# One planned order for a gated S4D convolution and spectral filter: fixed places in SBUF and PSUM, every instruction listed by the kernel, convolution pairs over 128 lanes

## The chip, the cores and the metric

The kernel runs on one core of a Trainium2 chip. Five engines work side by side: TensorE (PE, with its weight loads as PEld), VectorE (DVE), ScalarE (ACT), GpSimd (POOL) and SyncE (SP, which here only issues DMAs). Each runs its own instructions strictly in the order in which they stand in the program, and waits on semaphores for the others. The metric is the time of one execution on the device, in microseconds (us).

## The reference

Two branches are computed from one input `u` (1 x 2048 x 640) and mixed by a gate. In numpy's words, cut to what matters:

```python
g = sigmoid((x * gate_w).sum(-1))                       # one gate per time step
A = -exp(log_A_real) + 1j * A_imag                      # 640 channels x 128 states
P = exp((A * dt)[:, :, None] * arange(2048))            # powers of each state
K = 2 * einsum("dn,dnl->dl", (C_real + 1j*C_imag) * dt, P).real
a = irfft(rfft(u_t, 4096) * rfft(K, 4096))[:, :2048] + u * D_skip
b = irfft2(rfft2(x) * (w_r + 1j * w_i), s=(2048, 640))  # global filter
out = g * a + (1 - g) * b
```

## The kernel before

All Fourier transforms are matrix products with tables. The kernel has these stages; the letters are used below.

- **A** (`phase_a`, first half): for each of four column groups `c` (160 channels), `stage1` (L353, 80 products of 128 columns) and `stage2` (L366, 66 products of 160 columns) give the spectrum of `u`, which goes to DRAM as `u_d` (L448). L435 adds the gate's sums.
- **P** (`phase_p`): DVE and POOL compute the parameters of the 640 x 128 states, split them into three bf16 parts and write them to DRAM (`px_d`, `py_d`, `pm_d`).
- **K** (`phase_b`): the response of the state space model, in 40 tiles, in 8 blocks of 5. A tile takes two magnitude products (`mags`, L686) and two exponentials (L688), two sets of turns (`phases`, L696, six bf16 products of 512 columns) with two sines (L703 for the outer turns, L715 in place in PSUM for the inner ones), POOL products `y` (L706), three DVE products `x` (L718, L719, L720) and 32 small products `p_k` (`kgen`, L735). ACT changes its table between exponentials and sines, so that each block has one stretch of exponentials and one of sines. The turns and magnitudes share two double banks of PSUM (`bank2`), so that the five inner turns of a block use the two in turn.
- **F** (`phase_a`, second half, from L462): the two-dimensional filter, 9 rounds, each with a load of `u_d`, transposes (L533), products (L487, L492), the DVE's product with the filter (`filt`), and the way back (L598), ending in `s3e_d` in DRAM.
- **C** (`phase_c`, `phase_d`): for each column group, `stage1` and `stage2` of K (L353, L366), products with `u_d` on DVE (`ma`, `mb`, L830, L831), their sums `t2` (L835, L836), the way back (L849), a trip through DRAM (`s3_d`, written at L858, read by `load_c` at L901 as tile `t3`, four loads of 32 partitions that are four apart), and the last step: L170 for F's part, L928 for C's part, with the gate on DVE.

A product of the way back has 128 rows: `t2` holds the real part on partitions 0 to 63 and the imaginary part on 64 to 127. DVE and POOL make it out of `ma` and `mb`, whose partitions hold two values of k, in four instructions over 64 partitions each (L835, L836).

Order: tile pools give and take buffers, and generators are merged by shares of time (`merge`, L240, L978): A, F and the first part of C in one stream, P and K in the other; F begins when A has ended and C's main part when K has ended. DMAs are issued from SP, ACT (L817, L858) and POOL (L290, L663 to L671, L936). `t3`, `t3e`, `u` and the other tiles are separate buffers.

Of the kernel before, what the change touches and what calls it, by code (L numbers as in the profile page):

```python
# [11 lines left out]
I32 = mybir.dt.int32  # L12
# [11 lines left out]
NP = 33  # L24
MAGIC = 12582912.0
# [3 lines left out]

# [13 lines left out]
def _tables():  # L51
# [34 lines left out]
    w3 = np.swapaxes(w2, 1, 2) * wk[:, None, None]  # L86
    w2[K0, 64:] = 0.0
# [79 lines left out]
def halved(nc, out, w, x):  # L167

    for i in (0, 64):
        nc.tensor.matmul(out[i:i + 64], w[:, i:i + 64], x, start=True, stop=True)  # L170


def merge(*streams):

    live = [[0.0, t, g] for t, g in streams]
    while live:
        s = min(live, key=lambda x: x[0] / x[1])
        try:
            s[0] += next(s[2])
        except StopIteration:  # L180
            live.remove(s)
# [831 lines left out]
```

## Time and profile before

| | us |
|---|---|
| median of 3 runs (636.74 to 640.0) | 639.94 |
| the profiled execution | 637.14 |
| its span, first to last instruction | 635.3 |
| PE busy in the span | 535.0 (84%) |
| DVE busy | 452.3 (71%) |
| ACT busy | 310.5 (49%) |
| POOL busy | 313.7 (49%) |

The mean clock that TensorE was granted is 0.937 of full speed; 101.84 MB pass through the DMA queues. By the timeline, the first exponential's table load stands at 59.0 us, F works from 147 to 374 us, the last product of K ends at 468.2 us and the last L849 at 617.9 us. A view of windows gives the busy time of each engine in a stretch; a view of lines groups equal instructions with their total and mean time; the timeline gives single rows with their start.

### The profile page before, as it was taken

Reading aid. Unit: us, or ns where it says so; the run is one execution under the profiler, and the core shown is the slowest. Engines: PE = TensorE matmul, PEld = TensorE weight load, DVE = VectorE, ACT = ScalarE, POOL = GpSimd, SP = SyncE. Lnnn points to the kernel's source line nnn. Section 1 sums busy time; section 2 is a strip of 40 time slices with the busy share of each in tenths; the row PEclk is TensorE's granted clock in tenths of the full one; section 3 lists DMA queues with packets and bytes.
Section 4 is the critical chain, followed back from the end, with each engine's and each line's share of the span. In section 5 each row is a group of like instructions: output and inputs, shape, how many; then the busy total and the mean of one; then the engine's idle time right before and its main releaser. Section 6 shows DMA issues by size and latency. Waiting matters only on the chain. (4 is left out here: it accounts for less than half of the span.)

```text
span 635.3 us, 17319 instructions
## 1 busy us (share of the span) xinstructions
PE 535.0 (84%) x7432; PEld 379.6 (60%) x7432; DVE 452.3 (71%) x684; ACT 310.5 (49%) x476; POOL 313.7 (49%) x345
## 2 busy tenths in 40 slices
PE   8696999979984998498998978666687999999875
PEld 6594667647653775265665646333376878876651
DVE  6991487479999798489669705242479698796965
ACT  4564634524871486445773876848531323222120
POOL 4975561563585144803292374170724346546533
PEclk9897999989996799889899999887789999999999
DMA  9776223354354134021420258200044889969767
GB/s 344 301 267 245 79 90 118 114 171 142 86 192 120 42 101 141 8 79 44 162 78 24 63 175 311 94 2 2 1 152 156 300 272 309 359 202 324 255 217 269
DMA packets 49332, 101.84 MB, mean 160 GB/s; under 512 B 4756, under 2 KB 34216, under 8 KB 47624
## 3 DMA queue, kind: packets, MB, share of 16 engines
q1 hardware_dynamic: 24888, 67.08, 30.7%
q10 hardware_dynamic: 20080, 22.52, 11.1%
q0 software_dynamic: 4288, 11.15, 5.3%
q8 instruction: 58, 0.95, 0.6%
q14 instruction: 18, 0.15, 0.1%
HBM read 60.91 MB, written 39.81 MB: 159 GB/s over the span
## 5 line engine op out<-in xcount | busy, mean ns | idle before, releaser
L706 POOL TENSOR_TENSOR y<-e,sc 128x512 f32<-128x512 f32 x80 | 106.3, 1359 | 40.8 <-ACT sc L703 40.7
L366 PE MATMUL p_s<-t,w 128*64 128x160 f32 x1056 | 94.4, 317 | 9.8 <-ACT ut L400 5.4
L366 PEld LDWEIGHTS p_s<-t,w 128*64 128x64 f32 x1056 | 76.6, 140 | 23.9 <-ACT ut L400 6.3
L735 PE MATMUL p_k<-x,y 128*32 128x64 f32 x2560 | 58.9, 239 | 35.4 <-DVE x L719 28.4
L696 PE MATMUL p_p<-tr,pxy 64*128 64x512 bf16 x480 | 77.3, 410 | 6.6 <-ACT sc L703 4.5
L735 PEld LDWEIGHTS p_k<-x,y 128*32 128x32 f32 x2560 | 46.2, 120 | 54.9 <-issue 39.9
L718 DVE SCALAR_TENSOR_TENSOR x<-e,p_p 128x512 f32<-128x512 f32 x40 | 27.3, 682 | 61.9 <-ACT p_p L715 61.8
L688 ACT ACTIVATE e<-p_e 128x1024 f32<-128x1024 f32 x80 | 62.3, 816 | 9.1 <-PE p_e L686 5.8
L715 ACT ACTIVATE p_p<-p_p 128x1024 f32<-128x1024 f32 x40 | 40.4, 1010 | 39.4 <-PE p_p L696 32.9
L354 ACT COPY t<-p_s 128x512 f32<-128x512 f32 x40 | 24.9, 621 | 66.8 <-PE p_s L353 41.2
L835 POOL TENSOR_TENSOR t<-ma 64x320 f32<-64x320 f32 x32 | 28.0, 876 | 54.4 <-DVE ma L830 52.3
L703 ACT ACTIVATE sc<-p_p 128x1024 f32<-128x1024 f32 x40 | 40.5, 1024 | 19.7 <-PE p_p L696 13.0
L720 DVE TENSOR_TENSOR x<-e,p_p 128x1024 f32<-128x1024 f32 x40 | 48.6, 1215 | 0.0
L849 PE MATMUL p_i<-t,w 128*64 128x160 f32 x528 | 43.2, 303 | 4.4 <-POOL t L836 3.4
L353 PE MATMUL p_s<-c,kt 128*64 128x128 f32 x640 | 43.2, 274 | 3.8 <-DVE mb L831 2.0
L353 PEld LDWEIGHTS p_s<-c,kt 128*64 128x64 f32 x640 | 37.9, 136 | 13.4 <-issue 8.2
L589 POOL TENSOR_TENSOR qq<-z 128x320 f32<-128x320 f32 x17 | 16.9, 992 | 57.3 <-DVE z L586 56.0
L696 PEld LDWEIGHTS <-pxy 64*128 64x128 bf16 x480 | 22.4, 98 | 38.0 <-issue 29.0
L849 PEld LDWEIGHTS p_i<-t,w 128*64 128x64 f32 x528 | 37.0, 138 | 9.3 <-POOL t L836 4.0
L353 PE MATMUL p_s<-c,u 128*64 128x128 f32 x640 | 41.5, 277 | 0.2 <-DMA u<-in_u_l 0.2
L851 ACT COPY s<-p_i 128x640 f32<-128x640 f32 x32 | 21.7, 693 | 39.5 <-PE p_i L849 34.6
L353 PEld LDWEIGHTS p_s<-c,u 128*64 128x64 f32 x640 | 35.8, 137 | 6.8 <-issue 5.0
(159 smaller groups left out, 1066.9 us busy)
## 6 DMA issues: line engine op xcount, KB each, us to landing
u_d<-ut SPq DMA_DIRECT2D x32, 320.0 KB, 3.6
us<-u_d ACTq DMA_DIRECT2D x16, 640.0 KB, 6.4
s_d<-s ACTq DMA_DIRECT2D x15, 640.0 KB, 6.3
t<-s_d SPq DMA_DIRECT2D x14, 640.0 KB, 5.6
ww<-in_w_l SPq DMA_DIRECT2D x8, 642.0 KB, 3.9
ue<-u_d SPq DMA_DIRECT2D x8, 640.0 KB, 4.3
k_d<-kt SPq DMA_DIRECT2D x4, 1280.0 KB, 4.7
kt<-k_d SPq DMA_DIRECT2D x8, 640.0 KB, 5.6
```

The lines of the kernel that those rows point to most:

```text
L353: nc.tensor.matmul(p[64 * ri:64 * ri + 64, j, :], src(i + j), e1[ri], start=True, stop=True)
L366: ins = nc.tensor.matmul(p[64 * j:64 * j + 64, i, 160 * ri:160 * ri + 160], w2[:, x, 64 * ri:64 * ri + 64], t1[:, x // 2 if x < 32 else K0 ...
L688: st.exp = S.activation(ef[:, :, c:c + n], p[:, :, :n], AF.Exp)
L696: P.matmul(p[:, h, :], pars[t][1][l, v], turns[v][l, s], start=s == 0, stop=s == 2)
L703: T.trig = st.trig = S.activation(sc.rearrange("p v (h d) i -> p h v (d i)", h=2), p.rearrange("p h (v c) -> p h v c", v=2), AF.Sin, scale ...
L706: G.tensor_tensor(out=y[:, v], in0=es[t][:, :, 64:96], in1=sc[:, 1 - v], op=ALU.mult)
L715: T.trig = st.trig = S.activation(p[:, :, :], p[:, :, :], AF.Sin, scale=TWO_PI)
L718: V.scalar_tensor_tensor(out=x[:, 1, :, 32:64], in0=e[:, :, 32:64], scalar=-1.0, in1=sc[:, 0], op0=ALU.mult, op1=ALU.mult)
L720: V.tensor_tensor(out=x[:, 0].rearrange("p d (h j) -> p d h j", h=2), in0=e[:, :, 0:64].rearrange("p d (h j) -> p d h j", h=2), in1=sc[:, ...
L735: P.matmul(st.pb[32 * r:32 * r + 32, o, :], y[:, ri, 4 * qq + JR[r], :], x[:, ri, 4 * qq + JR[r], :], start=t % 2 + qq + 1 - ri == 0, stop ...
L835: (G if j else V).tensor_tensor(out=t2[0:64, o, :], in0=ma[l, :hn, 0, :], in1=ma[l, :hn, 1, :], op=ALU.subtract)
L849: T.mm = P.matmul(p[x:x + 64, i // 2, 160 * (i % 2):160 * (i % 2) + 160], T.w3[:, k0 + h + i, x:x + 64], t2[:, h + i, :], start=True, stop ...
```

## The change

The kernel is written anew around a planner. All buffers are slices of one SBUF tile `sb` of 53200 words a partition and one PSUM tile `ps` of 8 banks, at places fixed by the program (`Pool`, `Space`, `Banks`). The engines' calls are recorded (`Plan`, `Engine`) with what each reads and writes; `order` lays all of them out in time by estimates of their lengths, greedily and by the longest way to the end, and `emit` issues them in that order. `merge` and the waits on an instruction of another stream are gone. The framework below, which puts in the semaphores, is the same; it now sees every buffer as a part of `sb` or `ps`.

What is computed in each stage stays, with these differences:

- All DMAs are issued from SP.
- The turns of cosines and sines come from one layout of 52 rows (`pp_d` in the place of `px_d` and `py_d`); they are products as before. A tile's outer and inner turns now follow each other, and with two double banks (`pair`) taken in turn, the outer ones always use banks 3 and 4 and the inner ones banks 5 and 6.
- C's way back takes pairs over 128 lanes: `t2` is made by two DVE instructions over 128 partitions (L988, L989), and the product has tiles of 64 rows by 64 columns, 16 for a pair of k in the place of 8 of 128 rows (L997, with its table `t_w3c`). POOL has no part in C any more.
- F's part of the output is gated on ACT, an image row at a time (L1017), C's part on DVE (L1033); both take their PSUM from one bank (`bl`, bank 7). `t3` is one buffer at a fixed place (`t3p`); its four loads are L1024.

The diff, cut to its core (of the planner, its choice of the next instruction):

```diff
-            ga, gl = chain(phase_a(tc, A, T), phase_c(tc, A, T, cctx)), left()
-            next(gl)
-            next(ga)
-            next(gl)
-            while T.pin is None:
-                next(ga)
-            merge((194.0, ga), (76.8, gl))
-            phase_d(tc, A, T, cctx, out)
...
+        sb = top.enter_context(tc.tile_pool(name="sb", bufs=1)).tile([128, WIDE], F32, name="sb")
...
+        R = Plan(tc, sb[:, :], ps[:, :, :])
...
+        Y.dma_start(c1[:, 0:256], A["t_c1"][:, 0:256])
+        columns_head(T, A)
+        Y.dma_start(c1[:, 256:nc1], A["t_c1"][:, 256:nc1])
+        R.tag = "P"
+        params(T, A)
+        R.tag = "A"
+        columns(T, A)
+        R.tag = "K"
+        responses(T, A)
+        R.tag = "F"
+        spectral(T, A)
+        R.tag = "C"
+        convolution(T, A, out)
+        R.emit(order(R.units, OPT))
...
+    def emit(self, order):
+        with self.tc.manual_schedule():
+            for u in order:
+                for p, f, a, k in u.calls:
+                    p(f, a, k)
...
+    rank = {u: u.tail + bias.get(u.tag, 0.0) for u in units}
...
+    while len(out) < len(units):
...
+            s = [(start(u), u) for u in r]
+            s0 = min(x[0] for x in s)
+            lim = max(s0, free[e]) + slack.get(e, 100.0)
+            pick = None
+            for x, u in s:
+                if x > lim:
+                    continue
+                v = rank[u] - (x - s0)
+                if e == "PE" and u.mode != mode:
+                    v -= opt.get("hold", 300.0)
+                if e == "ACT" and u.table and u.table != table:
+                    v -= opt.get("table", 3000.0)
+                if pick is None or v > pick[0]:
+                    pick = v, x, u
+            if best is None or pick[1] < best[0]:
+                best = pick[1], pick[2]
...
+    out.sort(key=lambda u: u.at)
+    return out
...
+    def __call__(self):
...
+        self.n += 1
...
+        ap = self.plan.sb[:, b:b + (n if self.dt != BF16 else n // 2)]
...
-        nl, us = st.nl, st.us
...
-            V.tensor_tensor(out=ma[:nl, :hn], in0=pv, in1=uu, op=ALU.mult)
-            V.tensor_tensor(out=mb[:nl, :hn], in0=pv, in1=uu[:, :, ::-1, :], op=ALU.mult)
-            for j in range(nj):
-                l = slice(64 * j, 64 * j + 64)
-                o = slice(nj * h + j, nj * (h + hn), nj)
-                (G if j else V).tensor_tensor(out=t2[0:64, o, :], in0=ma[l, :hn, 0, :], in1=ma[l, :hn, 1, :], op=ALU.subtract)
-                (V if j else G).tensor_tensor(out=t2[64:128, o, :], in0=mb[l, :hn, 0, :], in1=mb[l, :hn, 1, :], op=ALU.add)
...
-            for i in range(hn):
-                for x in (0, 64):
-                    T.mm = P.matmul(p[x:x + 64, i // 2, 160 * (i % 2):160 * (i % 2) + 160], T.w3[:, k0 + h + i, x:x + 64], t2[:, h + i, :], start=True, stop=True)
...
+        p = b2()
+        with block(R):
+            for i in range(n):
+                stage2(T, p, t1, pr + i, i)
...
+        ma, mb, t2, s3 = wk(), wk(), t2p(), s3p()
+        V.tensor_tensor(out=ma[:nl, :n], in0=pv, in1=us, op=ALU.mult)
+        V.tensor_tensor(out=mb[:nl, :n], in0=pv, in1=us[:, :, ::-1, :], op=ALU.mult)
+        V.tensor_tensor(out=t2[:nl, 0, :n], in0=ma[:nl, :n, 0], in1=ma[:nl, :n, 1], op=ALU.subtract)
+        V.tensor_tensor(out=t2[:nl, 1, :n], in0=mb[:nl, :n, 0], in1=mb[:nl, :n, 1], op=ALU.add)
+        q = bi()
+        with block(R):
+            for ri in range(2):
+                for i in range(n):
+                    for j in range(nl // 64):
+                        for x in (0, 64):
+                            l = slice(64 * j, 64 * j + 64)
+                            P.matmul(q[x:x + 64, j, 160 * i:160 * i + 160], w3[l, pr + i, ri, x:x + 64], t2[l, ri, i, :], start=ri + i == 0, stop=ri == 1 and i == n - 1)
+        if n == 2:
+            S.copy(s3.rearrange("p i j d -> p j i d"), q[:, :, 0:320].rearrange("p j (i d) -> p j i d", i=2))
+            Y.dma_start(T.s3_d[c, 4 * pr:4 * pr + 8].rearrange("(x k) a d -> (k a) x d", k=2),
+                        s3.rearrange("p i j d -> p (i j) d"), writes=[("s", c, pr // 4), ("r33", c)] if pr == 8 else [("s", c, pr // 4)])
...
-                T.ld = eng.dma_start(t3s[c][y::4, :, a:a + w], src[:, :, a:a + w])
...
-                halved(nc, p[:, 0:n], T.e3e, t3es[c][:, a + i:a + i + n])
-            V.tensor_tensor(out=oe[:, i:i + n], in0=p[:, 0:n], in1=gate(1, a + i, n), op=ALU.mult)
...
+    b1, b2, bi, bl = Banks(R, [0]), Banks(R, [1, 3], 2), Banks(R, [5], 2), Banks(R, [7])
...
+    def even(c):
+        te, oe = tep(), oep()
+        Y.dma_start(te, T.s3e_d[c].rearrange("k (r a) d -> (k r) a d", r=4), reads=[("e", k) for k in range(16)] + [("e1",)])
+        for a, n in AS:
+            p = bl()[:, 0:160 * n].rearrange("p (a d) -> p a d", a=n)
+            with block(R):
+                for i in (0, 64):
+                    P.matmul(p[i:i + 64], T.e3e[:, i:i + 64], te[:, a:a + n], start=True, stop=True)
+            for j in range(n):
+                S.activation(oe[:, a + j], p[:, j], AF.Copy, scale=T.gate[:, 1, a + j:a + j + 1])
+        return oe
+    def last(c, oe):
+        t3 = t3p()
+        for y in range(4):
+            src = T.s3_d[c, 16 * y:16 * y + 16].rearrange("k (j x a) d -> (k j) x a d", x=2, j=2)
+            Y.dma_start(t3[y::4], src, reads=[("s", c, y)] + [("r33", c)] * (y == 2))
...
+        for k, (a, n) in enumerate(AS):
...
+            p = bl()[:, 0:160 * n].rearrange("p (a d) -> p a d", a=n)
+            with block(R):
+                for x in range(2):
+                    P.matmul(p[64 * x:64 * x + 64], T.e3, t3[:, x, a:a + n], start=True, stop=True)
+            for j in range(n):
+                V.scalar_tensor_tensor(out=ot[:, a % 8 + j], in0=p[:, j], scalar=T.gate[:, 0, a + j:a + j + 1], in1=oe[:, a + j], op0=ALU.mult, op1=ALU.add)
+            if k % 3 == 2:
+                Y.dma_start(out[c, :, a - 6:a + 2], ot)
...
-        p = phases(t, 0)
-        sc = p.rearrange("p v (d i) -> p v d i", d=16)
-        with after(st.exp):
...
+        p = pair()
...
+                    P.matmul(p[:, h, :], st.pp[l, zz], turns[l, v, s], start=s == 0, stop=s == 2)
+        u = S.activation(p if o is None else o, p if o is None else p.rearrange("p h (v c) -> p h v c", v=2), AF.Sin, scale=TWO_PI)
+        u.pre.update(dict.fromkeys(st.exps, 1))
...
+        turned(zz, 1, sc.rearrange("p v (h d) i -> p h v (d i)", h=2))
+        for v in (1, 0):
+            G.tensor_tensor(out=y[:, v], in0=e[:, :, 64:96], in1=sc[:, 1 - v], op=ALU.mult)
+        p = turned(zz, 0, None)
...
+    for b in range(0, 40, BT):
+        load(b // BT)
+        st.exps, st.new = [], []
+        es = [mags(zz) for zz in range(BT)]
+        for zz in range(BT):
+            x, y = phases(zz, es[zz])
+            kgen(b + zz, x, y)
+        st.sins = st.new
```

Three places show how the order moves. First SP, from the start of the program; each row is one DMA, target and source, and its size. Before:

```order
L258 DMA ld<-in_ld_l 128x5
L407 DMA u<-in_u_l 128x384
L407 DMA u<-in_u_l 128x896
L407 DMA u<-in_u_l 128x1280
L262 DMA cr<-in_cr_l 128x640
L262 DMA ci<-in_ci_l 128x640
L262 DMA ai<-in_ai_l 128x640
L262 DMA lar<-in_la_l 128x640
L427 DMA w_70<-in_t_w 128x4224
```

And now (`in_t_w` is the table of `stage2`, `in_cr_l` the first of the parameters):

```order
L649 DMA sb<-in_u_l 128x512
L501 DMA sb<-in_t_c 128x256
L649 DMA sb<-in_u_l 128x768
L503 DMA sb<-in_t_c 128x355
L656 DMA sb<-in_gw_l 128x160
L649 DMA sb<-in_u_l 128x1280
L666 DMA sb<-in_t_w 128x1408 x3
L669 DMA sb<-in_u_l 128x1280
L532 DMA sb<-in_cr_l 128x640
L532 DMA sb<-in_ci_l 128x640
```

The parameters' loads have moved behind the table of `stage2` and another half column group of `u`.

Second TensorE, where K's first magnitudes stand among A's products. Before (L686 magnitudes, L366 and L353 of A, L696 the first turns; one of several like stretches):

```order
L353 MATMUL p_s_865<-c_67,u 64x128 x8
L686 LDWEIGHTS pm
L686 MATMUL p_e<-tr,pm 128x512
...
L353 MATMUL p_s_884<-c_67,u 64x128 x8
L696 LDWEIGHTS pxy_76
L696 MATMUL p_p<-tr,pxy_76 128x512
...
L353 MATMUL p_s_917<-c_67,u 64x128 x8
```

And now, in the third of A's four column groups (L636 is `stage2`, L626 `stage1`, L890 the magnitudes):

```order
L636 MATMUL ps<-sb 64x160 x48
L890 LDWEIGHTS sb
L890 MATMUL ps<-sb 128x512
...
L636 MATMUL ps<-sb 64x160 x12
...
L636 MATMUL ps<-sb 64x160 x6
L626 MATMUL ps<-sb 64x128 x56
L678 MATMUL ps<-sb 32x64 x20
L626 MATMUL ps<-sb 64x128 x24
L890 LDWEIGHTS sb
```

The first turns (now L902) stood among A's products of the third group; now they stand behind all but six products of A's fourth and last group.

Third, C, with the semaphores that each row waits for (DMAHW and a number: a DMA's landing; the other names: an engine's progress). Before, TensorE around the first L170 of a group:

```order
L849 MATMUL p_i_6516<-t_6278,w_4557 64x160 x7
L366 MATMUL p_s_6533<-t_6041,w_70 64x160 [waits DVE_49]
L366 MATMUL p_s_6533<-t_6041,w_70 64x160 x7
L170 MATMUL p_e<-t3e,c_67 64x480 [waits DMAHW0_49]
L170 MATMUL p_e<-t3e,c_67 64x480
L353 MATMUL p_s_6555<-c_67,kt 64x128 [waits Activation_49]
```

Now SP at the four loads of `t3` of the second group:

```order
L1000 DMA s_d<-sb 128x4x160 [waits DMAHW0_49,Activation_49]
L1024 DMA sb<-s_d 32x5120 [waits DMAHW1_49,DMAHW3_49,DVE_49,DMAHW7_49,PE_49,Activation_49]
L1024 DMA sb<-s_d 32x5120 [waits DMAHW2_49]
L1024 DMA sb<-s_d 32x5120
L1024 DMA sb<-s_d 32x5120 [waits DMAHW6_49,DMAHW4_49]
L1035 DMA out<-sb 128x1280 [waits DMAHW5_49,DVE_49]
```

And TensorE at the same place (L1015 reads `te`, F's part, and the table `e3e`; no row here reads `t3`):

```order
L997 MATMUL ps<-sb 64x160 x7
L626 MATMUL ps<-sb 64x128 [waits Activation_49]
L626 MATMUL ps<-sb 64x128 x7
L1015 MATMUL ps<-sb 64x480 [waits DMAHW3_49,DMAHW4_49,DMAHW2_49,DMAHW7_49,DMAHW1_49,DVE_49]
L1015 MATMUL ps<-sb 64x480
L636 MATMUL ps<-sb 64x160 x8
```

The load of F's part was the one DMA that L170 waited for; L1015 now waits for five DMAs, and four of them are the four loads of `t3` above (they stand on the semaphores 1 to 4), which L1015 does not read. The first load of `t3` in turn waits for PE, DVE and ACT.

More of the change, by code (lines that the diff above doesn't have):

```diff
@@ L1 @@
 import math
-from contextlib import ExitStack, nullcontext
+import sys
+from contextlib import ExitStack, contextmanager
 import numpy as np
@@ L164 @@
     pass
[L167 to L181, printed above, removed]
-def run(gen):
-    for _ in gen:
-        pass
-def chain(*gens):
-    for g in gens:
-        yield from g
+OPT = {}
@@ new lines, in stage1, with stage2 @@
+def stage1(T, bank, e1, src, q0, nq, t1, copy):
+    t1v = t1.rearrange("p x d y -> p d x y")
+    for i in range(0, nq, 4):
+        p = bank().rearrange("p (q x) -> p q x", q=4)
+        with block(T.R):
+            for j in range(4):
+                for ri in range(2):
+                    T.P.matmul(p[64 * ri:64 * ri + 64, j, :], src(i + j), e1[ri], start=True, stop=True)
+        copy(t1v[:, 4 * (q0 + i):4 * (q0 + i) + 16], p.rearrange("p q (j x y) -> p (q j) x y", j=4, y=2))
+def stage2(T, p, t1, pr, i):
+    nl = 128 if pr < 16 else 64
+    for ri in range(2):
+        for j in range(nl // 64):
+            x = 2 * pr + j
+            T.P.matmul(p[64 * j:64 * j + 64, i, 160 * ri:160 * ri + 160],
+                       T.w2[:, x, 64 * ri:64 * ri + 64], t1[:, x // 2 if x < 32 else K0 // 2, :, x % 2], start=True, stop=True)
@@ new lines, in columns @@
+                    P.matmul(p[x:x + 32], zz[:, q, :], u[:, q, :], start=q < 4, stop=q > 15)
+            S.copy(T.lg[:, 2 * c + h, :], p)
+        for pr in range(0, 17, 2):
+            n = min(2, 17 - pr)
+            nl = 128 if pr < 16 else 64
+            ut = T.aut()
+            for i in range(n):
+                p = bank().rearrange("p (i x) -> p i x", i=1)
+                with block(R):
+                    stage2(T, p, t1, pr + i, 0)
+                src = p[:nl, 0, 0:320].rearrange("p (r d) -> p r d", r=2)
+                (V.tensor_copy if i else S.copy)(ut[:nl, i], src)
+            Y.dma_start(T.u_d[c, :nl, pr:pr + n], ut[:nl, :n], writes=[("u", c, pr + i) for i in range(n)])
@@ L526, in transposes @@
+    def transposes(src, dst, nl, back):
+        for c, (e0, e1) in enumerate(CH):
+            p = bank()
+            with block(R):
                 for x in range(4):
@@ new lines, in kgen @@
+    def kgen(t, x, y):
+        c, i = t // 10, 4 * (t % 10 - 1)
+        if t % 2 == 0:
+            st.pb = pk().rearrange("p (i a) -> p i a", i=8)
+        with block(R):
+            for qq in range(4):
+                o = 4 * (t % 2) + qq
+                for ri in (1, 0):
+                    for r in (0, 1, 2, 3):
+                        P.matmul(st.pb[32 * r:32 * r + 32, o, :], y[:, ri, 4 * qq + JR[r], :], x[:, ri, 4 * qq + JR[r], :],
+                                 start=t % 2 + qq + 1 - ri == 0, stop=t % 2 + qq - ri == 4)
+        if t % 2:
+            kt = pkt()
+            S.copy(kt, st.pb)
+            V.tensor_tensor(out=kt[:, :, 31], in0=kt[:, :, 31], in1=T.dsk[:, c, i:i + 8], op=ALU.add)
+            Y.dma_start(T.k_d[c, :, i:i + 8], kt, writes=[("k", c, i // 4), ("k", c, i // 4 + 1)])
```

1268 lines of the change are left out of this document (623 added, 645 removed).

## The prediction

> **What bounds the kernel now.** I read the page's busy times first, then the windows by stage, then the groups of lines, and last single rows of the timeline where one stage hands over to the next.
>
> ```profile
> PE 535.0 (84%) x7432; PEld 379.6 (60%) x7432; DVE 452.3 (71%) x684; ACT 310.5 (49%) x476; POOL 313.7 (49%) x345
> core 0: us, PE busy (x) PEld busy (x) DVE busy (x) ACT busy (x) POOL busy (x), PEclk, DMA share, GB/s
> 0.00:59.00 59.00, 45.22 (x716) 38.76 (x716) 42.68 (x54) 29.77 (x58) 42.56 (x49) 0.95 0.81 304
> 59.00:147.00 88.00, 82.31 (x1452) 57.10 (x1451) 55.60 (x93) 42.50 (x51) 40.78 (x45) 0.96 0.35 117
> 147.00:374.00 227.00, 194.66 (x2212) 129.88 (x2214) 183.87 (x294) 135.47 (x228) 106.20 (x123) 0.93 0.29 89
> 374.00:468.00 94.00, 67.44 (x1329) 39.51 (x1325) 35.81 (x45) 61.23 (x74) 40.85 (x40) 0.85 0.26 92
> 468.00:618.00 150.00, 134.56 (x1692) 111.40 (x1684) 125.19 (x176) 40.99 (x67) 77.57 (x85) 0.99 0.81 269
> 618.00:635.30 17.30, 10.78 (x48) 2.95 (x44) 9.12 (x23) 0.58 (x1) 5.74 (x5) 0.89 0.72 247
> ```
>
> TensorE's 84% hides stages with different limits. In F with K (147 to 374) it is busy for 195 of 227 us and DVE for 184; in the rest of K (374 to 468) nobody is busy for more than 72%, since one tile's chain runs from engine to engine; in C (468 to 618) TensorE is busy for 135 of 150. So before the change K without cover loses most, and C is bound by TensorE.
>
> **The beginning.** The order on SP puts 3840 words of `u`, 611 of `t_c`, 160 and all 4224 of `in_t_w` ahead of `in_cr_l`: 8835 words a partition, 4.5 MB, where 2565 words stood, and 0.4 MB more on other queues. That is 2.8 MB more.
>
> ```profile
> 58.11 1.00 PE L686 MATMUL p_e<-tr,pm 48*128 48x512 bf16 x4 [5.64 <-DMA pm<-pm_d]
> ```
>
> The first magnitudes waited for the parameters even before. At the first window's 304 GB/s, 2.8 MB are 9 us: first magnitudes at 67 (bounds: 58, if the parameters are late through DVE and POOL alone; 76 at half that rate).
>
> ```profile
> L353 PE MATMUL p_s<-c,u 128*64 128x128 f32 x640 | 41.5, 277 | 0.2 <-DMA u<-in_u_l 0.2
> L366 PE MATMUL p_s<-t,w 128*64 128x160 f32 x1056 | 94.4, 317 | 9.8 <-ACT ut L400 5.4 <-ACT t L354 1.6 <-DVE mb L831 1.5
> L435 PE MATMUL p_g<-u,z 128*32 128x64 f32 x320 | 7.3, 222 | 0.1
> ```
>
> A column group of A costs (41.5 + 94.4/2 + 7.3)/4 = 24 us (L366 serves A and C alike). By the order on TensorE, the rest of the third group and nearly all of the fourth stand between the first magnitudes and the first turns, 1.2 groups by its counts: 29 us, so the first turns come at 97.
>
> **K and F together.** From there on K and F share the engines, and DVE has the most to do.
>
> ```profile
> L718 DVE SCALAR_TENSOR_TENSOR x<-e,p_p 128x512 f32<-128x512 f32 x40 | 27.3, 682 | 61.9 <-ACT p_p L715 61.8
> L719 DVE TENSOR_TENSOR x<-e,p_p 128x512 f32<-128x512 f32 x40 | 27.2, 680 | 0.0
> L720 DVE TENSOR_TENSOR x<-e,p_p 128x1024 f32<-128x1024 f32 x40 | 48.6, 1215 | 0.0
> ...
> 147.00:374.00 227.00, 20.64 (x17) 0.93 0.29 89
> ```
>
> The last row is the window of F, with L720 alone: 17 tiles of K lie in it. A tile's three products take 2.58 us. F's own DVE work is 183.9 - 17 x 2.58 = 140 us, K's 40 tiles are 103: 243 in all. By the order DVE gets the last seven tiles only after F's last operation, so 243 - 18 = 225 stand ahead. Before, F's stretch ran at 184/227 = 0.81 of DVE; now all 33 tiles are laid out over it by one list, and more work is at hand at any time. Bounds are 0.81 (278 us) and 1 (225); I take 0.87, nearer to the row, for 259: F's end at 356.
>
> ```profile
> 425.90 0.82 PE L696 MATMUL p_p<-tr,pxy 64*128 64x512 bf16 x6
> 426.82 1.01 ACT L715 ACTIVATE p_p<-p_p 128x1024 f32<-128x1024 f32 x1 [0.18 <-PE p_p L696]
> 428.07 0.68 DVE L718 SCALAR_TENSOR_TENSOR x<-e,p_p 128x512 f32<-128x512 f32 x1
> 428.67 0.68 DVE L719 TENSOR_TENSOR x<-e,p_p 128x512 f32<-128x512 f32 x1
> 429.27 1.22 DVE L720 TENSOR_TENSOR x<-e,p_p 128x1024 f32<-128x1024 f32 x1
> ```
>
> The seven tiles go by this chain: inner turns into the bank, the sine in place, three products that read it; from 425.90 to 430.49, 4.6 us. Before, the next tile's inner turns had the other bank pair; now all of them use banks 5 and 6, so the chain cannot overlap: 7 x 4.6 = 32. Between them lies one block's stretch of exponentials:
>
> ```profile
> L688 ACT ACTIVATE e<-p_e 128x1024 f32<-128x1024 f32 x80 | 62.3, 816 | 9.1 <-PE p_e L686 5.8
> L688 ACT ACT_TABLE_LOAD x8 | 10.3, 1283 | 7.1 <-issue 7.0
> ```
>
> 62.3/8 = 7.8 for one block, two table loads of 1.3, and 1.5 to hand over: 12. K ends at 97 + 259 + 44 = 400, against 468 before: this is what the change gains.
>
> **C's body.** I start from the 150 us of before and change these terms.
>
> ```profile
> L353 PE MATMUL p_s<-c,kt 128*64 128x128 f32 x640 | 43.2, 274 | 3.8 <-DVE mb L831 2.0 <-DMA kt<-k_d 1.5 <-ACT s L851 0.4
> ...
> L849 PE MATMUL p_i<-t,w 128*64 128x160 f32 x528 | 43.2, 303 | 4.4 <-POOL t L836 3.4 <-DVE mb L831 1.0
> ...
> 99.59 1.36 PE L366 MATMUL p_s<-t,w 128*64 128x160 f32 x16
> 100.88 1.10 PE L735 MATMUL p_k<-x,y 128*32 128x64 f32 x64
> ...
> 487.77 1.26 PE L849 MATMUL p_i<-t,w 128*64 128x160 f32 x16
> 488.86 1.31 PE L366 MATMUL p_s<-t,w 128*64 128x160 f32 x16
> ```
>
> By the order, 3.5 blocks of 16 products of `stage1` and 24 of `stage2` stand ahead of K's end: 3.5 x 16 x 43.2/640 + 24 x 94.4/1056 = 6 us. The wait for POOL's half of `t2` goes (up to 4.4). F's part of the last group moves to the end (4 of TensorE's time here, counted below). L997 is 16 products of half the rows where L849 had 8, at the same time if four tiles run side by side as two did. But the array changes its shape: 16 products before a change of shape take 1.29 us from start to start, and 1.09 without one, 0.2 for a change; C has 73 new changes, +14 (0 to 14). C's body: 150 - 6 - 4 - 4 + 14 = 150.
>
> **The new waits in C.** TensorE's L1015 waits for the four loads of `t3`, which it does not read, and the first of the loads waits for PE, DVE and ACT. So all three stop: the load starts when the last of their instructions ahead of it ends, and L1015, with 8 products of `stage2` and all that follows queued behind it in TensorE's order, starts when the data has landed. DVE and ACT have the same wait at their next instruction, and DVE's `t2` and ACT's copies are what TensorE would need next, so no other engine covers it. By the order there are seven such places: the four loads of the first group one by one, those of the second and of the third group four at once, and three of the last group; its fourth load is an eighth, in the end of the program, and counted there.
>
> ```profile
> t<-s_d SPq DMA_DIRECT2D x14, 640.0 KB, 5.6
> out<-ot SPq DMA_DIRECT2D x3, 640.0 KB, 3.9
> ```
>
> One load takes 5.6 us from issue to landing and another transfer of its size alone 3.9; four are 2.6 MB, at 304 GB/s 8.6 us and 2 for the start. With 0.9 for the semaphores, a single one is 6.5, four 11, three 9: 4 x 6.5 + 2 x 11 + 9 = 57. Bounds: 45 (the four at 3.9 + 0.9 and the others at 9, 9, 8) and 85 (transfers of `s_d` and `out` in the same queues, half as long again).
>
> ```profile
> 191.70:200.00 8.30, 0.01 (x1) 0.00 (x0) 8.27 (x6) 0.69 (x3) 6.76 (x8) 0.80 0.50 144
> 200.00:213.70 13.70, 12.97 (x107) 9.16 (x110) 10.06 (x20) 3.54 (x6) 2.65 (x4) 0.50 0.12 47
> ...
> 261.30:270.00 8.70, 0.00 (x0) 0.02 (x1) 2.16 (x4) 0.33 (x1) 6.50 (x11) 0.71 0.06 14
> 270.00:275.10 5.10, 5.09 (x77) 3.77 (x77) 4.06 (x5) 0.58 (x1) 0.00 (x0) 0.50 0.26 66
> ```
>
> After a gap of over 8 us the granted clock was 0.50, for 13.7 us in one case and 5.1 in the other: a loss of 2.6 to 6.9 us. I take the lower one, since TensorE in C is as dense behind the gap as there: 7 x 2.6 = 18 (to 48). [...]
>
> **The end.**
>
> ```profile
> 625.19 1.04 PE p_c L928 x4
> ...
> 626.25 0.98 DVE ot L931 x3
> ...
> 627.37 0.77 PE p_c L928 x4
> ```
>
> Products into a bank and the gating out of it take 627.37 - 625.19 = 2.2 us for a group of columns, if one bank serves them all, as bank 7 now does for L1015 and L1031. The last group's F part is six such groups ahead of the fourth load, 12 (ACT's rows in place of DVE's), the wait for that load 5, six groups for C's part 12, and the last output takes 3.9: 33 in all, where the last window has 17.3 (bounds 26, if ACT's and DVE's rows overlap, and 40).
>
> **Sum.** 400 + 150 + 57 + 18 + 33 = 658 for the span, and 1.8 (637.14 - 635.3) around it: 660. The profiled execution lies 2.8 below the median shown, which is within what measurements of this kernel scatter (0.5%: the bound for telling a change from none), so I forecast 662.
>
> **Rivals.** (1) *The list packs K and F up to DVE's limit* (faster). Then F ends at 97 + 225 = 322, K at 366, 34 us sooner: 628. It turns faster than before only if DVE is busy for over 0.95 of the stretch from 97 (225/236, 23 us less than my 259). For it: orders are made over all stages, and 40 tiles are independent. Against: 0.81 now, single banks for inner turns, and TensorE's own 0.86 there. (2) *The waits for `t3` cost nothing*, because engines have work that stands ahead of them: 662 - 57 - 18 = 587. Against: L1015's row in the order names these loads' semaphores, and each engine keeps its order. (3) *K keeps its pace*: its windows run from 59 to 468, 409 us; from 67 that gives 476, 76 later than I say: 738. For it: the inner turns' single bank. Against: much of the 409 was A's and F's. (4) *Four 64 x 64 tiles don't run side by side*: L997 would take twice 43.2, so 705.
>
> ```profile
> L492 PE MATMUL p_d<-td,ft 64*64 64x161 f32 x8 | 1.5, 310 | 0.0
> ```
>
> Such a shape occurs here eight times only; 1.5 us for 8 products is 0.19 each, where 528 of L849 have 0.08 each, so the trace doesn't exclude it. [...] That the change doesn't do what it says is no rival, as each engine runs the listed order.
>
> **How the numbers follow.** My forecast has 0.50 (own range 640 to 690: 45 to 85 and 18 to 48 against a denser K), rival 1 0.22, rival 2 0.08, rival 3 0.10, rival 4 0.10. From 606 to 714 the range leaves out rivals 2 and 3 and little else, 0.2. Faster: rivals 1 and 2, 0.30 together; within 0.5%, 0.06, from where the forecast and rival 1 meet; slower 0.64.
>
> **What would show it.** Right: the first magnitudes (L890) near 67 and first turns (L902) near 97; DVE about 0.87 busy from there until F's end; K's last product (L933) near 400; seven gaps of 6 to 13 us on TensorE in C ahead of L1015 or `stage2`, ended by the DMA from `s_d`, with a granted clock of 0.50 behind them; L997 at 43 us; about 33 us from the last gap's load to the end. Wrong: L997 at 80 or more (rival 4), DVE idle for a quarter from 97 on (rival 3), gaps of 1 or 2 us in C (rival 2). The largest step on which all hangs is that K and F gain 68 and C loses 75; either may be off by 30.

## The result, and the profile after

The changed kernel takes 655.86 us (median of 4 runs, 654.21 to 660.19) and the kernel before 638.34 beside it (636.01 to 640.0): the ratio is 1.0288, with a 95% interval from 1.0223 to 1.0352. It is 17.5 us slower. The profiled execution has a span of 654.2 us.

First the page of the changed kernel: busy times, and the granted clock in 40 slices.

```profile
PE 531.0 (81%) x7956; PEld 373.3 (57%) x7956; DVE 397.9 (61%) x724; ACT 350.3 (54%) x572; POOL 178.9 (27%) x159
...
PEclk9878999898999989999999989976879979869655
```

TensorE is busy for about as long as before (535.0 us) in a longer span, and the granted clock, 0.99 over C before the change (468 to 618 us), now drops in the last third of the program. The windows of the changed kernel, cut at the four places that the prediction names (first turns, F's last operation on DVE, K's last product, the landing that ends the last gap), in the columns of the table of before:

```profile
111.20:363.70 252.50, 229.44 (x3444) 150.76 (x3441) 230.16 (x400) 199.67 (x305) 133.49 (x121) 0.98 0.33 103
363.70:406.90 43.20, 39.39 (x858) 26.66 (x850) 21.94 (x37) 31.56 (x42) 15.81 (x13) 0.96 0.40 133
406.90:617.10 210.20, 150.24 (x2128) 110.67 (x2129) 91.94 (x189) 60.19 (x113) 0.00 (x0) 0.85 0.61 198
617.10:654.20 37.10, 20.27 (x48) 3.58 (x48) 5.22 (x16) 5.22 (x16) 0.00 (x0) 0.50 0.17 65
```

K ends at 406.9 us, 61 us earlier than before; from there to the end it takes 247 us, where it took 167 (635.3 - 468.2). So 61 us are gained and 80 lost behind it. Where they are lost stands in the view of waits, here for TensorE from 406.9 us on (the sum, the number of waits, the longest):

```profile
PE ps L1015 <- DMA sb<-s_d: 41.8, 4, 13.5
PE ps L636 <- DMA sb<-s_d: 16.3, 3, 7.3
PE ps L1031 <- DVE sb L1033: 6.2, 6, 1.1
```

Seven waits for loads of `t3` out of `s_d`, 58.1 us together, at L1015 and `stage2` (L636), neither of which reads `t3`. One of them in the timeline (the number behind the start is the length of a row; in brackets what the engine waited for):

```profile
514.52 1.32 PE L997 MATMUL ps<-sb 64*64 64x160 f32 x32
515.36 2.42 SPq L1024 DMA_DIRECT2D sb<-s_d  x4
...
515.78 1.09 PE L626 MATMUL ps<-sb 128*64 128x128 f32 x16
517.89 0.54 SPq L1035 DMA_DIRECT2D out<-sb  x1
526.81 0.70 ACT L999 COPY sb<-ps 128x640 f32<-128x640 f32 x1 [13.03 <-DMA sb<-s_d]
526.83 0.83 DVE L986 TENSOR_TENSOR sb<-ps,sb 128x640 f32<-128x640 f32 x1 [12.67 <-DMA sb<-s_d]
...
526.95 1.87 PE L1015 MATMUL ps<-sb 128*64 128x480 f32 x4 [10.08 <-DMA sb<-s_d]
```

Three engines come back within 0.14 us of each other, each at an instruction that does not read what was loaded. Behind the gap TensorE runs at half clock for 4.6 us more (windows of the changed kernel):

```profile
516.90:526.90 10.00, 0.00 (x0) 0.00 (x0) 0.07 (x1) 0.09 (x1) 0.00 (x0) 0.72 0.86 303
526.90:531.50 4.60, 4.55 (x28) 3.50 (x30) 2.80 (x5) 2.30 (x5) 0.00 (x0) 0.50 0.24 80
531.50:540.00 8.50, 8.50 (x136) 6.28 (x134) 4.20 (x8) 5.42 (x12) 0.00 (x0) 1.00 0.39 118
```

### The profile page after: what moved, and what is told of

Read it like the earlier page. It is cut to its first block, busy times and chain, and to the rows that moved or that the text cites. A ratio compares the mean times of both kernels' runs of the same rounds, so it can differ in the third digit from the quotient of the medians.

```text
span 654.2 us, 18460 instructions
## 1 busy us (share of the span) xinstructions
PE 531.0 (81%) x7956; PEld 373.3 (57%) x7956; DVE 397.9 (61%) x724; ACT 350.3 (54%) x572; POOL 178.9 (27%) x159
## 4 chain that ended last, share of the span: by engine, by line
PE 46%; DVE 25%; DMA 11%; ACT 7%; issue 4%; SPq 1%; POOL 0%; DVEq 0%; ACTq 0%
PE ps L636 11%; PE ps L626 8%; DMA sb<-s_d 7%; PE ps L997 5%; DMA sb<-u_d 5%; PE ps L1015 4%; PE ps L902 4%; DVE sb L920 4%; PE ps L933 3%; PE ps L726 3%; PE ps L1031 3%; ACT sb L891 2%; DVE sb L918 2%; DVE sb L917 2%; PE ps L827 2%
## 5 line engine op out<-in xcount | busy, mean ns | idle before, releaser
L912 POOL TENSOR_TENSOR sb<-sb 128x512 f32<-128x512 f32 x80 | 108.9, 1387 | 100.4 <-ACT sb L903 96.2
L636 PE MATMUL ps<-sb 128*64 128x160 f32 x1056 | 96.5, 326 | 31.6 <-DMA sb<-s_d 16.3
L636 PEld LDWEIGHTS ps<-sb 128*64 128x64 f32 x1056 | 79.7, 144 | 50.5 <-issue 14.5
L626 PE MATMUL ps<-sb 128*64 128x128 f32 x1280 | 88.4, 289 | 5.5 <-DMA sb<-in_t_c 3.8
L626 PEld LDWEIGHTS ps<-sb 128*64 128x64 f32 x1280 | 77.7, 145 | 14.8 <-issue 5.4
L902 PE MATMUL ps<-sb 52*128 52x512 bf16 x480 | 72.4, 395 | 13.0 <-ACT sb L903 6.8
L627 ACT COPY sb<-ps 128x512 f32<-128x512 f32 x80 | 53.6, 673 | 47.1 <-PE ps L626 47.1
L1015 PE MATMUL ps<-sb 128*64 128x480 f32 (+1 forms) x96 | 30.5, 716 | 46.8 <-DMA sb<-s_d 41.8
L891 ACT ACTIVATE sb<-ps 128x1024 f32<-128x1024 f32 (+1 forms) x80 | 62.5, 830 | 5.3 <-PE ps L890 5.0
L689 DVE COPY sb<-ps 128x320 f32<-128x320 f32 x32 | 15.5, 489 | 61.6 <-PE ps L636 39.8
L920 DVE TENSOR_TENSOR sb<-sb,ps 128x512 f32<-128x512 f32 x80 | 51.0, 678 | 0.0
L726 PE MATMUL ps<-sb 128*128 128x161 f32 (+3 forms) x280 | 48.6, 316 | 1.5 <-DVE sb L814 1.5
L997 PE MATMUL ps<-sb 64*64 64x160 f32 x1056 | 49.2, 319 | 0.5 <-DVE sb L988 0.5
L902 PEld LDWEIGHTS <-sb 52*128 52x128 bf16 x480 | 24.1, 97 | 41.2 <-issue 28.5
L997 PEld LDWEIGHTS ps<-sb 64*64 64x64 f32 x1056 | 37.6, 141 | 16.3 <-issue 10.2
L1033 DVE SCALAR_TENSOR_TENSOR sb<-ps,sb 128x160 f32<-128x160 f32 x64 | 20.8, 377 | 41.2 <-issue 27.8
```

Source lines behind the costliest of these rows:

```text
L626: T.P.matmul(p[64 * ri:64 * ri + 64, j, :], src(i + j), e1[ri], start=True, stop=True)
L627: copy(t1v[:, 4 * (q0 + i):4 * (q0 + i) + 16], p.rearrange("p q (j x y) -> p (q j) x y", j=4, y=2))
L636: T.P.matmul(p[64 * j:64 * j + 64, i, 160 * ri:160 * ri + 160], T.w2[:, x, 64 * ri:64 * ri + 64], t1[:, x // 2 if x < 32 else K0 // 2, :, ...
L726: P.matmul(p[:, 161 * i:161 * i + n], lhs(i, part), tab(i)[part][0], start=i == 0, stop=False)
L891: u = S.activation(ef[:, :, c:c + n], p[:, :, :n], AF.Exp)
L902: P.matmul(p[:, h, :], st.pp[l, zz], turns[l, v, s], start=s == 0, stop=s == 2)
```

## The experiments

**1. The loads of `t3` without gaps between the partitions.** The tile and the table `e3` are laid out so that each load goes to 32 neighbouring partitions. The instructions of every engine and their order stay the same.

```diff
-        e1[0], e1[1], e3.reshape(4, 32, 64).swapaxes(0, 1).reshape(128, 64), e3e.reshape(128, 128), np.eye(128), one,
+        e1[0], e1[1], e3.reshape(128, 64), e3e.reshape(128, 128), np.eye(128), one,
...
-            Y.dma_start(t3[y::4], src, reads=[("s", c, y)] + [("r33", c)] * (y == 2))
+            Y.dma_start(t3[32 * y:32 * y + 32], src, reads=[("s", c, y)] + [("r33", c)] * (y == 2))
```

> The changed kernel with one difference: the four loads of t3 go to 32 partitions that follow each other (32y to 32y+31) in place of partitions four apart, and the rows of the table e3 stand in the same order. Every engine has the same instructions in the same order; in the listing, L1015 and stage2 no longer wait for these loads, and the loads no longer wait for DVE and ACT. Theory A (the waits are the cause of the loss): the seven gaps of 58.1 us in all go, and with them the half clock behind them, half of the 31.6 us in which TensorE was busy at clock 0.50 between 429 and 620 us, 15.8; the end at full clock gives 5 more: 655.9 - 79 = about 577 us (570 to 587). Theory B (C would lose the time elsewhere, for instance waiting for t3 or for s_d through the one DMA queue): a gain of less than 40, above 615 us. Theory C (these waits cost nothing, rival 2 of the prediction turned round): 650 to 660.

Measured: 589.86 us (588.73 to 593.9), ratio to the kernel before 0.9282 (0.9235 to 0.9329). That is 66 us less than the changed kernel, and 7% less than the kernel before. TensorE's waits from K's end (410.4 us) to the end of the span, and the windows of C:

```profile
PE ps L1031 <- DMA sb<-s_d: 8.0, 1, 8.0
PE ps L1031 <- DVE sb L1033: 6.2, 6, 1.1
PE ps L1015 <- ACT sb L1017: 5.0, 5, 1.1
```

```profile
407.00:560.00 153.00, 144.16 (x2250) 105.99 (x2248) 95.39 (x194) 66.61 (x130) 0.00 (x0) 1.00 0.92 274
560.00:588.70 28.70, 10.79 (x28) 1.89 (x28) 5.22 (x16) 0.68 (x2) 0.00 (x0) 0.54 0.28 96
```

The seven gaps are gone, and the one wait left for `s_d` is L1031's, which does read `t3`. The clock in C is 1.00 up to 560 us. Apart from where these loads write, the two programs have the same instructions in the same order, so the waits are the cause of the loss, as theory A has it. Theory A had 79 us for it; the gain is 66, and 589.86 lies 3 above its range. From K's end to the last L997 it takes 138.1 us (410.4 to 548.5) where the changed kernel took 200.0 (406.9 to 606.9): 61.9 less, of which six gaps are 48.6; the rest, 13.3, is put down to the low clock and the restart behind them. The seventh gap (9.5) is paid back in part: what stands behind it waits 8.0 us for its own load now, as against 1.9. The full clock at the end, for which theory A had 5 us, did not come either (0.54 from 560 us on).

**2. The gaps filled with products.** To separate a gap from the low clock behind it, six of the seven gaps were filled with products of a small tile of its own, for which `sb` was made 64 words shorter; the control has the shorter `sb` and the small tile, without the products.

```diff
-WIDE = 53200
-RIGHT = 23210
+WIDE = 53136
+RIGHT = 23146
...
+        for _ in range(WARM[R.n]):
+            R.nc.tensor.matmul(R.ps[0:64, 5, 320:448], R.warm[:, 0:64], R.warm, start=True, stop=True)
```

> The changed kernel with the SBUF tile shorter by 64 words and a small tile of its own beside it that nothing uses: the control for gaps_filled. 655.9 us, give or take 4, with seven gaps on TensorE of 58 us in all and a granted clock of 0.50 behind them, if their cause does not hang on the tile's length.

> As gaps_control, but in six of the seven gaps TensorE multiplies the small tile (bf16, 64 rows of weights columns by 128 columns, 90 to 170 products a gap) into a part of PSUM that nothing reads; the loads of t3 and all that waits for them stay. Theory A (the gap itself costs 58 us and the half clock behind it a further 15.8 in C): the clock stays at 1.0 over the gaps that are filled, and the time falls by 8 to 16 us against gaps_control. Theory B (the low clock behind the gaps costs nothing, since DVE or the DMA queue would be late there anyway): same within 4 us. If the products outlast a gap, the row of the first product behind it shows it, and that is to be added.

Measured: 676.8 us for the control and 676.07 with the products (2 runs each). So the control was no copy of the changed kernel: with 64 words less it took 21 us more, though every buffer has the same place in a row. Its waits on TensorE:

```profile
PE ps L997 <- DMA sb<-s_d: 24.2, 3, 11.7
PE ps L1015 <- DMA sb<-s_d: 21.3, 2, 12.6
PE ps L1015 <- DVE sb L1033: 17.9, 1, 17.9
PE ps L636 <- DMA sb<-s_d: 7.6, 1, 7.6
```

There are again seven gaps, now of 70.9 us, and one of them ends with DVE, whose own turn came late behind the load. In the listing of this program the first load of the second and of the third group waits for all eight DMA semaphores, where that of the changed kernel waited for three. What the strided loads are taken to touch thus hangs on the width of a row of `sb`; that is how many buffers in one tile can cost time though no buffer overlaps another. With the products, the gaps from one product of the kernel to the next, in the six places ahead of the last L997, are 62.7 us against 58.3 in the control, and the rest between K's end and the last L997 is 147.9 against 151.4: 3.5 us gained behind the gaps, 4.4 lost in them. The time is the one that theory B gives, but the products ended 3.4 to 9.0 us ahead of the end of each filled gap, so a part of each stayed open, and the mean granted clock was 0.912, between the 0.882 of the control and the 0.943 of experiment 1. So the run does not decide between its theories.

**3. Who sets the pace of K and F.** Two runs of the changed kernel with part of the work left out where the planned instructions are issued, so that their order stays:

```diff
+    if u.eng == "DVE" and u.tag == "K" and u.line == 920:
+        k = {n: v[..., 0:8] if isinstance(v, AP) else v for n, v in k.items()}
```

> The changed kernel, with three quarters of DVE's product L920 left out (80 instructions of 512 columns become 128; part of x stays unwritten, so K is not the response). DVE has about 80 x 0.5 = 40 us less to do between 111 and 407 us, all other engines the same work and order. Theory A (DVE sets the pace of K and F): the last product of K (406.7 us) comes 25 to 40 us earlier, total 616 to 631 us. Theory B (TensorE, 0.90 busy there, sets it): less than 10 us earlier, total 646 to 656. Between them: both engines share it, 12 to 24 us.

```diff
+    if u.eng == "PE" and u.line == 933:
+        R.n = (getattr(R, "n", -1) + 1) % 32
+        if R.n % 8 > 3 and not k["stop"]:
+            return
```

> The changed kernel, with nearly half of TensorE's products L933 left out (those with ri = 0 but the last ones; K is not the response). TensorE has about 1270 x 0.0175 = 22 us less to do between 111 and 407 us; DVE, ACT and POOL have the same work. Theory A (DVE sets the pace): the last product of K comes less than 6 us earlier, total 650 to 656 us. Theory B (TensorE sets it): 16 to 22 us earlier, total 634 to 640. Between: 7 to 15 us.

Measured: 640.82 us (8 runs, 636.86 to 643.61) with less work on DVE, 651.7 (2 runs) with less on TensorE. The windows from the first turns to F's end and on to K's end, first with less on DVE, then with less on TensorE:

```profile
108.70:348.00 239.30, 221.82 (x3404) 149.03 (x3404) 206.39 (x400) 198.80 (x304) 135.50 (x120) 0.99 0.34 108
348.00:389.50 41.50, 38.05 (x902) 26.41 (x894) 18.82 (x41) 31.88 (x43) 16.50 (x14) 1.00 0.42 141
```

```profile
108.80:363.00 254.20, 226.85 (x2520) 144.19 (x2521) 230.44 (x399) 199.99 (x305) 133.37 (x120) 0.94 0.32 100
363.00:404.20 41.20, 35.79 (x662) 23.36 (x658) 22.31 (x38) 31.75 (x42) 16.30 (x14) 1.00 0.43 144
```

With less on DVE, L920 took (shortest, median and longest in ns, first and last start):

```profile
L920 DVE TENSOR_TENSOR sb<-sb,ps x80: 269/279/282, 114.6 to 387.7; 128x128 f32<-128x128 f32 x80
```

It took 0.68 us before that, so DVE had 32 us less to do, not 40; from the first turns to K's end it took 280.8 us in the place of 295.7. DVE's work counts for about half (15 of 32). On TensorE 1120 of the 2560 instructions of L933 were left out, and the stretch stayed at 295.4. L933 alone over that stretch, in the changed kernel and then with less on TensorE (PE, PEld, clock, DMA):

```profile
111.20:406.90 295.70, 45.02 (x2560) 38.37 (x2560) 0.98 0.34 107
108.80:404.20 295.40, 29.48 (x1440) 22.84 (x1440) 0.95 0.33 106
```

L933 was busy for 15.5 us less, but the clock was lower (0.95 against 0.98), and all of TensorE's busy time fell by only 6.2 us (262.6 against 268.8). The 16 to 22 us of theory B did not come. Whether less work on TensorE would gain something at an unchanged clock, this run does not show.

**4. The inner turns in both bank pairs.** On top of experiment 1:

```diff
-        sc, x, y = pc(), px(), py()
+        sc, x, y = pc(), px(), py(); pair.n += zz % 2
...
-        p = turned(zz, 0, None)
+        p = turned(zz, 0, None); pair.n += zz % 2
```

> As t3_straight, with the two double banks of K dealt out otherwise: in every second tile the outer turns take banks 5 and 6 and the inner ones 3 and 4, so that the inner turns of neighbouring tiles no longer wait for one bank pair. All stages are planned anew. In t3_straight the first turns come at 111 us and K's last product ends at 410 us, and DVE waits 29 us for the inner sines. Theory A (the single pair of the inner turns keeps DVE at 0.92 of its time): DVE's waits for the inner sines fall by half or more and K ends 10 to 20 us earlier, total 570 to 580. Theory B (those waits come from the stretches of exponentials, in which no sine can run): within 4 us of 590. Theory C: later, since outer turns now wait for DVE's products: over 594.

Measured: 600.06 us (2 runs), 10 more than experiment 1. What DVE waits for over the whole span, in experiment 1 and then here:

```profile
DVE sb L917 <- ACT ps L903: 29.1, 15, 10.3
```

```profile
DVE sb L917 <- ACT ps L903: 34.9, 13, 14.7
```

The waits for the inner sines did not fall, and K ended at 416.8 us in the place of 410.4. Theory A falls. From K's first product to its last it takes 288.7 us as against 289.4, so K's pace did not change; the 6 us are lost ahead of the first product (128.1 us in the place of 121.1). The time is theory C's, and TensorE's waits for DVE at the turns (L902 behind L920) rose from 5.5 to 9.7 us, which is not enough for it. The longest single wait, 10 us and more, is as long as a block's stretch of exponentials (9.6 us of L891 with its table load), as theory B has it, but no run took such a stretch away, and the new plan is another order in other places too; what sets the other half of K's pace stays open.

**5. C's way back with 128 rows again.** On top of experiment 1, `t2` in four instructions of 64 partitions (half on POOL), and products of 128 rows:

```diff
+                (G if j else V).tensor_tensor(out=t2[0:64, :n, j], in0=ma[l, :n, 0], in1=ma[l, :n, 1], op=ALU.subtract)
+                (V if j else G).tensor_tensor(out=t2[64:128, :n, j], in0=mb[l, :n, 0], in1=mb[l, :n, 1], op=ALU.add)
...
-                            P.matmul(q[x:x + 64, j, 160 * i:160 * i + 160], w3[l, pr + i, ri, x:x + 64], t2[l, ri, i, :], start=ri + i == 0, stop=ri == 1 and i == n - 1)
+                            P.matmul(q[x:x + 64, j, 160 * i:160 * i + 160], w3[:, k // 2, k % 2, x:x + 64], t2[:, i, j, :], start=True, stop=True)
```

> As t3_straight, with C's way back as it was in the kernel before: t2 in four instructions of 64 partitions, half on DVE and half on POOL, and products of 128 rows (264 pairs of halves in the place of quadrants, table t_w3). C from K's end (410 us) to the last product of the way back (548.5) takes 138 us in t3_straight. Theory A (the 73 changes of the array's shape cost 0.13 to 0.2 us each): the products get 8 to 14 us cheaper, and C ends 4 to 14 us earlier if POOL's part of t2 is ready in time. Theory B (POOL's 64-partition parts of 0.88 us make TensorE wait, as L849 did for 3.4 us in the kernel before): within 4 us, or later.

Measured: 592.31 us (2 runs) against 589.86; no difference that two runs can tell. C from K's end to the last product of the way back takes 133.2 us (417.6 to 550.8), 5 less than in experiment 1. But the new plan ends K 7 us later, and 16 instructions each of `stage1` and of the way back, 2.2 us, now stand ahead of that end. The windows of C, in experiment 1 and then here:

```profile
410.40:548.50 138.10, 135.07 (x2130) 101.70 (x2126) 91.31 (x187) 59.65 (x112) 0.00 (x0) 1.00 0.93 282
417.60:550.80 133.20, 125.25 (x1564) 104.98 (x1564) 110.57 (x181) 58.02 (x110) 58.46 (x65) 0.97 0.96 289
```

TensorE is busy for 9.8 us less, of which 2.2 only moved, so the quadrants cost it 7.6, or a little more, since the clock was lower here (0.97 against 1.00); it waits 5 us more than in experiment 1 (8.0 against 3.0), which takes most of that back. In experiment 1's timeline one sees where the quadrants cost:

```profile
481.41 1.33 PE L636 MATMUL ps<-sb 128*64 128x160 f32 x16
482.67 1.32 PE L997 MATMUL ps<-sb 64*64 64x160 f32 x32
483.92 1.09 PE L626 MATMUL ps<-sb 128*64 128x128 f32 x16
...
485.65 1.32 PE L636 MATMUL ps<-sb 128*64 128x160 f32 x16
486.81 1.04 PE L626 MATMUL ps<-sb 128*64 128x128 f32 x16
```

16 products of `stage2` take 1.26 us from start to start ahead of L997, 1.16 ahead of `stage1`; L997's 32 take 1.25, where L849's 16 took 1.09. Over the 33 pairs of k that is 33 x (0.10 + 0.16) = 8.6 us, or 0.12 for each of the 73 changes, an estimate from these rows.

**6. The parameters' loads first, and two banks at the end.** Both on top of experiment 1, alone and together:

```diff
-OPT = {}
+OPT = {"bias": {"P": 200000.0}}
```

```diff
-        oe = even(c)
-        last(c, oe)
+        bl.banks = [7, 0] if c == 3 else [7]
+        oe = even(c); last(c, oe)
```

> As t3_straight (589.9 us), but the plan gives the stage of the parameters the highest rank, so that their loads stand first on SP, ahead of u and the tables. Theory A (the parameters' late loads delay K, as the prediction has it): the first magnitudes come 10 us or more earlier than 84.6 us, the first turns near 97 instead of 111, and the total falls to 573 to 582. Theory B (A's own work on TensorE, which starts with u and stands ahead of the first turns in the order, sets them): magnitudes may come earlier, but u comes later by the parameters' 2.8 MB, so the first turns stay at 111 or come later, up to 120: total 588 to 600.

> As t3_straight (589.9 us), with the last column group's even part and last step dealt out to PSUM banks 7 and 0 in turn (stage1 has left bank 0 by then) in place of bank 7 alone; planned anew. Theory A (one bank makes product and gating take turns, 2.2 us for each group of columns, as the prediction counts it): six groups of the last step, 2.5 us each now, fall to the longer of the two, about 1.5, so the stretch from the last load of t3 to the end falls by about 6, and the total by 5 to 12. Theory B (the low clock or the load decide there): within 3 us.

> straight_params and straight_tail2 together, t3_straight under both. If their gains add: 589.9 plus what each of them changes, within 4 us; else the plan moved something that hides one of them.

Measured (4 runs each): 602.34 us (598.33 to 604.33) with the parameters first, 587.76 (586.17 to 590.45; ratio to the kernel before 0.9240, 0.9191 to 0.9289) with two banks, 597.02 (596.47 to 597.45) with both. The rows of the run with the parameters first, with the start of the first and the last of a line (behind the three durations in ns):

```profile
L890 PE MATMUL ps<-sb x160: 266/326/387, 67.1 to 391.2; 50*128 50x512 bf16 x80, 50*128 50x256 bf16 x80
```

```profile
L902 PE MATMUL ps<-sb x480: 372/377/631, 113.1 to 414.5; 52*128 52x512 bf16 x160
```

The first magnitudes come at 67 in the place of 84.6, and the first turns no earlier: 113. A's products set them, as theory B has it, and these now start late, behind the parameters' loads (the first at 13.4 us in the place of 3.8). The time is 2 us above theory B's range. K's first product comes at 121.1 us with and without this change; the plan is another one throughout, and K ends 9 us later (419.3), for which no run gives the reason. With two banks, the last step in the windows of experiment 1 and then of this run:

```profile
568.70:588.70 20.00, 10.09 (x24) 1.72 (x24) 5.22 (x16) 0.00 (x0) 0.00 (x0) 0.50 0.16 66
```

```profile
570.90:584.40 13.50, 7.60 (x24) 2.05 (x24) 5.13 (x16) 0.00 (x0) 0.00 (x0) 0.75 0.24 97
```

It falls by 6.5 us as theory A says, at a clock of 0.75 in the place of 0.50, so that the second bank is not shown to be the whole cause; but L1031 waits 10 us for the last load in the place of 8, and the medians lie only 2.1 apart, less than their spreads. The two gains and losses nearly add (589.86 + 12.5 - 2.1 = 600.2; measured 597.02). The version with two banks is the fastest that was run; it isn't told from experiment 1 by these runs.

## Why the prediction was right, and where its steps were not

The forecast of 662 us is 6 above the measured 655.86, and its cause, loads of `t3` that stop three engines, is shown by experiment 1. Step by step, in the profiled execution:

| step | forecast us | measured us |
|---|---|---|
| first turns | 97 | 111.2 |
| from there to F's end | 259 | 252.5 |
| the last seven tiles | 44 | 43.2 |
| C's body without the waits | 150 | 137 to 138 |
| seven waits for `t3` | 57 | 58.1 |
| half clock behind them | 18 | 13 to 15 |
| the end | 33 | 37.1 |
| span | 658 | 654.2 |

- **The first turns** are the step that failed: "That is 2.8 MB more", 9 us, was to bring the magnitudes to 67, and the turns 29 us later. The magnitudes came at 84.6, and the parameters' loads did not set them. The first block's loads were issued by 68 us, and TensorE came to the magnitudes out of A's products without a wait (no bracket behind the row):

```profile
67.64 0.80 SPq L880 DMA_DIRECT2D sb<-pm_d  x2
...
77.48 7.15 PE L636 MATMUL ps<-sb 128*64 128x160 f32 x96
84.57 0.39 PE L890 MATMUL ps<-sb 50*128 50x512 bf16 x2
```

Experiment 6, with the magnitudes at 67 and the turns at 113, agrees. So the 9 us were the wrong term: the forecast had to count A's products ahead of the magnitudes. And A itself lost time that I hadn't counted. TensorE's waits up to 111 us were:

```profile
PE ps L636 <- ACT sb L689: 7.7, 1, 7.7
PE ps L636 <- DVE sb L689: 6.6, 3, 3.8
PE ps L626 <- DMA sb<-in_t_c: 3.8, 1, 3.8
```

ACT's and DVE's copies (L689) stand in these engines' order behind steps of the parameters, 14 us in all.

- **K and F** came out as forecast: DVE was busy for 230.16/252.5 = 0.91 of the stretch, where I took 0.87. The reason given was half right: DVE's work counts for half of what is taken from it, and for TensorE's no gain was seen, at a lower clock (0.95 against 0.98, experiment 3). The last seven tiles took 43.2 us, but the reason given for their length, the single bank pair, did not hold where it was tried (experiment 4, over all tiles), and no row shows the 1.5 us to hand over by themselves: they were an estimate of mine.
- **C's body** was mis-sized by 12 to 13. I subtracted 4 of TensorE's waits of before, those for POOL; all of them went. The view of waits of the kernel before, for TensorE from 468 to 618 us, begins with

```profile
PE p_e L170 <- DVE oe L911: 4.9, 6, 0.9
PE p_i L849 <- POOL t L836: 3.4, 2, 1.8
PE p_s L353 <- DVE mb L831: 2.0, 1, 2.0
```

and sums to 15.3 us; in experiment 1 it is 3.0 up to the last L997, with no gap over 0.4 us up to 534 us. Whether the new order or the gating on ACT does this, no run separates. And the changes of shape came to 8.6 by experiment 5's rows, where I had 14: my 0.2 for a change compared 1.29 of L366 with 1.09 of L849, and 16 products of `stage2` without a change take 1.16.
- **The waits** were right in place, number and sum: singles 6.9, 7.3, 2.1 and 8.7 (forecast 6.5 each), fours 10.1 and 13.5 (11 each), the three 9.5 (9). No row shows the 2 us for a start and the 0.9 for the semaphores by themselves; what is shown are the whole waits.
- **The half clock** comes to 13.3 us by experiment 1 for six gaps, 2.2 each where I took 2.6; by the windows of the changed kernel, half of the 29.6 us of TensorE's work at clock 0.50 that stand behind them is 14.8. Experiment 2 could not separate it from the restart. At clock 0.50 L997's 32 products took 2.34 us from start to start (449.12 to 451.46), at 1.00 they take 1.25; 4.6 us at 0.50 stood behind the gap shown above, and half of them is 2.3.
- **The end** took 37.1 in the place of 33, since all of it ran at clock 0.50: six groups of the even part took up to 2.9 us each (617.12 to 620.04), 1.87 of them in L1015's four products, which took 0.98 at clock 1.00 (488.47), where I took the 2.2 of before, and the last load's wait shrank to 1.9.

Of the rivals, the second (no cost of the waits) and the third (K at its old pace) are refuted by the view of waits and by K's end. For the fourth, L997 has 49.2 us of busy time where L849 had 43.2:

```profile
L997 PE MATMUL ps<-sb 64*64 64x160 f32 x1056 | 49.2, 319 | 0.5 <-DVE sb L988 0.5
```

By experiment 5's rows 32 of its instructions take 1.25 us, the time of 18 of L849's, not of 32: one every 39 ns, where L849 had one every 68. That is near what four tiles side by side would give, and far from the rival's doubling. The first rival, DVE's limit, was not reached: 0.91, between my 0.87 and the 0.95 from which it would have turned the sign. The misses were 14 late, 7 and 1 early, 12 and 4 early, and 4 late; that they nearly cancel is luck, and the total is closer than its terms.

## What to carry to other kernels

When buffers become slices of one tile, look at the waits of the first instruction behind each strided load: a load over partitions that lie apart can be taken to touch much more of the tile than it writes, and the engines that use the tile then stop for it, here seven times and for 58.1 us of TensorE. Look for it in the order of the program, in waits for data that an instruction doesn't read; the cure is a layout in which each load goes to neighbouring partitions, here two lines and 66 us. And a new plan is judged stage by stage: this one was 61 us ahead at K's end and lost more behind it, and only without the false waits does its gain appear.

## What the hardware showed that was not expected

TensorE's busy share was a poor measure of its work: with 1120 instructions and 15.5 us of L933 less, its busy time from the first turns to K's end fell by only 6.2 us, while the granted clock went from 0.98 to 0.95. And sparse work did not bring the clock back: from 617.1 us on TensorE was busy for 20.3 of 37.1 us, in pieces of 1.3 to 1.9 us with gaps of about 1 us, and stayed at 0.50 to the end. In experiment 1 the same six even groups, with gaps of 0.8 to 1.1 us, began at full clock and kept it: the window from 550.0 to 560.7 us has 5.6 us of work at 1.00. With two banks the last step began at 0.50 but had no gaps (5.8 us of work from 570.9 to 576.7), and the clock was 1.00 from there to 583.5.
